# A window attention kernel: order of the LayerNorm transposes, place of the convolution, and the order of the setup

## The chip, the cores and the metric

The kernel runs on one core of one Trainium2 chip. The metric is device time in microseconds (us), the median of the runs. The core has five engines that run their own queues of instructions: TensorE (PE; its weight loads are shown apart as PEld), VectorE (DVE), ScalarE (ACT), GpSimd (POOL) and SyncE (SP, which only issues DMAs here). They meet through semaphores.

## The reference

An image x of 511 x 511 positions with 192 channels (bfloat16) goes through a depthwise 3 x 3 convolution that is added to it, a LayerNorm without weights over the channels, attention with 4 heads of 48 channels in windows of 7 x 7 positions, an output projection, and a residual sum:

```
pe  = sum over i, j of xpad[:, i:i+H, j:j+W, :] * dw_pe[i, j]     # 3 x 3, per channel
x0  = x + pe
h   = (x0 - mean(x0)) / sqrt(var(x0) + 1e-5)
qkv = windows(h) @ w_qkv                    # 73 x 73 windows of 49 tokens
out = softmax(q k^T * 48**-0.5) v           # per window and head
y   = x0 + unwindow(out @ w_o)
```

## The kernel before, in words

**Blocks and groups.** The 5329 windows are cut into 42 blocks of up to 128 windows. In X (three rotating buffers) a window is a partition and its 49 x 192 values lie along it. Attention works on groups of 8 windows: 16 groups in a block, 11 in the last, 667 in all.

**Convolution.** XP holds for each window of a block its 9 x 9 patch, with the 81 positions on the partitions. T holds for each channel an 81 x 49 matrix made of the 9 taps. One matmul per channel (conv_mm, L298) loads the channel's 81 x 128 patch values as weights and streams 49 columns of T. Ten channels fill a psum buffer psc (there are two), and VectorE casts them into X (L303). 192 matmuls make a block.

**LayerNorm.** VectorE adds x itself (ln_add, L310; the rows come by DMA into xs) and takes the statistics (ln_stat, L314). GpSimd makes 1/sqrt (L320, L321) and scales (ln_norm, L329). The mean is taken out through the weights. Then ln_tr (L336 to L355), seven times a block, transposes up to eight positions: for each half of the channels (kt = 0, 1) eight TensorE transposes of 128 x 96 into one of the two banks of a psum buffer ps, and a copy into HO, by VectorE for the first half and by ScalarE for the second.

**Attention of a group.** Stage A makes q and then k with four matmuls of 392 columns each (L364) and a cast on ScalarE (L372). Stage B makes the scores (L402) and the exponential (L410). Stage V makes v with eight matmuls of 192 columns (L380, cast L388). Stage D multiplies with v (L423), and VectorE divides by the sum (L432, L433). Stage E transposes the result back (L447) and copies it over the group's part of HO (L448). D runs one group later than A, E two groups later. proj (L453) multiplies four positions of a finished block with w_o (eight matmuls of 192 columns, L459), ScalarE casts (L463), GpSimd adds to X (L467), and SyncE stores.

**The order.** From the branch on (the logits are shown small enough, or else a slow path runs) the order of each queue is the order in which the Python code issues, so it is written by hand. In the loop over the groups it is: q, E, k, D, the proj calls that are due, ln_tr for the next block if one is due, B, V. While block b is in attention, block b + 1 is prepared: the convolution in the first 44% of the groups, the statistics from 46% to 82%, the transposes from 56% to 96%. The convolution's matmuls are put between others by fill(), which is called after each matmul of q, k, v and proj. It spreads the group's share over nlong calls, 16 plus 8 for each proj. hook() issues statistics, loads and stores. The loads of XP for the block after next begin when the convolution has left XP, from 44% to 92%. All psum work but the convolution takes the three ps buffers in turn, so the fourth user from here waits until the first one's readers are done.

**The setup.** Ahead of the branch, in an order that a scheduler works out from the dependencies, psum, XP and X are cleared, the selection matrix Sel is made by GpSimd, T is made by 49 small matmuls (L120) and copied out two positions at a time with single elements 98 bytes apart (L129), the weights are centred, and a value is computed that decides the branch. After the branch the patches of block 0 are loaded, its convolution runs alone, then its LayerNorm and transposes, and then the loop begins.

## Time and profile before

The time before is 5380.8 us, the median of two runs (5376.48 and 5385.11). The profiled execution has a span of 5361.9 us.

| engine | busy us | share of the span | instructions |
|---|---|---|---|
| TensorE matmuls | 4426.2 | 83% | 75049 |
| TensorE weight loads | 3610.8 | 67% | 75049 |
| ScalarE | 3054.3 | 57% | 3855 |
| VectorE | 2727.6 | 51% | 4190 |
| GpSimd | 2116.4 | 39% | 1188 |

The mean granted clock of TensorE is 0.777 of full speed; in the records it is either 0.50 or 1.00. The main DMA queue's packets take 27.9% of the span of the 16 DMA engines.

The columns: an engine is busy while an instruction of its own runs; a wait on a semaphore is idle time. Weight loads overlap matmuls. A matmul takes longer at the lower clock, so TensorE's busy time depends on its clock. Shares over the whole span are means over stages with different limits, so the stages have to be looked at one by one.

### The profile page before, as it was taken

The page shows a single profiled execution, that of the slowest core. Times are in us where ns is not written, and L with a number is a line of the kernel's source. Part 1 is how long each engine was busy: PE and PEld are TensorE (multiplying, and loading weights), DVE is VectorE, ACT ScalarE, POOL GpSimd, SP SyncE. Part 2 cuts the span into 40 slices and gives each one's busy share as a digit, 9 for nine tenths or more (in the row PEclk, how much of TensorE's full clock was granted, in tenths as well). Part 3 has the DMA queues.
Part 4 walks back from the last instruction along what each step waited for, and adds up shares of the span by engine and source line. Part 5 has one row for each costly group of instructions (what it writes and reads, how often), then busy time and mean ns, then how long its engine had stood idle before and what let it go on. Part 6 is the DMA issues. An engine that isn't in the chain of part 4 may idle for free. (4 is left out here: it accounts for less than half of the span.)

```text
span 5361.9 us, 167300 instructions
## 1 busy us (share of the span) xinstructions
PE 4426.2 (83%) x75049; PEld 3610.8 (67%) x75049; DVE 2727.6 (51%) x4190; ACT 3054.3 (57%) x3855; POOL 2116.4 (39%) x1188
## 2 busy tenths in 40 slices
PE   2688888888888888888888888888888888888777
PEld 1566776776766666677766766666667776676665
DVE  5554555455555544555545555545554555455542
ACT  1455555556555565556655555555555566555555
POOL 3433333334444433334433444433333343344333
PEclk9886787777777776778877777767777888777777
DMA  2222222233333222222323333222222233233221
GB/s 69 59 68 67 68 68 68 68 78 77 82 80 83 72 68 68 68 68 68 78 68 77 83 80 83 71 67 68 68 68 68 68 78 73 70 74 81 68 48 32
DMA packets 529706, 377.00 MB, mean 70 GB/s; under 512 B 454181, under 2 KB 454373, under 8 KB 528979
## 3 DMA queue, kind: packets, MB, share of 16 engines
q1 hardware_dynamic: 528531, 365.92, 27.9%
q8 instruction: 589, 9.65, 0.8%
q14 instruction: 138, 1.13, 0.1%
q10 hardware_dynamic: 448, 0.30, 0.0%
HBM read 265.31 MB, written 100.27 MB: 68 GB/s over the span
## 5 line engine op out<-in xcount | busy, mean ns | idle before, releaser
L467 POOL TENSOR_TENSOR X<-X,pO 128x768 bf16<-128x768 bf16 (+1 forms) x546 | 894.6, 1654 | 2789.2 <-ACT pO L463 2787.9
L364 PE MATMUL ps<-HO,Wqk 96*128 96x392 bf16 x5336 | 1639.4, 426 | 20.1 <-ACT HO L352 15.8
L298 PEld LDWEIGHTS <-XP 81*128 81x128 bf16 x8064 | 1246.8, 185 | 139.2 <-issue 51.6
L298 PE MATMUL psc<-T,XP 81*128 81x49 bf16 x8064 | 1303.1, 211 | 41.3 <-DMA xs<-in_x_dram 32.0
L380 PE MATMUL ps<-Wv,HO 96*128 96x192 bf16 x5336 | 863.4, 299 | 118.3 <-DVE o L433 112.2
L343 PE MATMUL ps<-ident,X 128*96 128x128 bf16 x4116 | 412.0, 253 | 640.9 <-DVE HO L352 592.0
L432 DVE RECIPROCAL rs<-ps 128x16 f32<-128x16 f32 x667 | 169.8, 255 | 1393.8 <-PE ps L423 896.8
L303 DVE CAST X<-psc 128x490 bf16<-128x490 f32 x840 | 542.8, 646 | 591.5 <-PE psc L298 585.0
L364 PEld LDWEIGHTS <-Wqk 96*128 96x128 bf16 x5336 | 623.7, 124 | 303.8 <-issue 238.1
L352 ACT COPY HO<-ps 96x1024 bf16<-96x1024 bf16 (+1 forms) x294 | 284.5, 968 | 869.7 <-PE ps L343 869.7
L343 PEld LDWEIGHTS <-X 128*96 128x96 bf16 x4116 | 336.8, 148 | 644.7 <-issue 598.6
L372 ACT CAST k<-ps 128x784 bf16<-128x784 f32 x667 | 543.6, 815 | 363.8 <-PE ps L364 269.6
L329 POOL TENSOR_TENSOR X<-X,rstd 128x1536 bf16<-128x1536 bf16 (+1 forms) x294 | 734.2, 2515 | 18.5 <-DMA out_dram<-X 5.4
L380 PEld LDWEIGHTS <-HO 96*128 96x128 bf16 x5336 | 604.6, 122 | 158.6 <-issue 111.7
L459 PE MATMUL ps<-Wo,HO 96*128 96x192 bf16 x4116 | 690.6, 302 | 16.3 <-ACT HO L448 12.7
L388 ACT CAST v<-ps 128x768 bf16<-128x768 f32 x667 | 535.7, 803 | 267.3 <-PE ps L380 218.7
L372 ACT CAST q<-ps 128x784 bf16<-128x784 f32 x667 | 543.7, 815 | 249.2 <-PE ps L364 240.9
L433 DVE TENSOR_TENSOR o<-ps,rs 128x768 bf16<-128x768 f32 x667 | 638.4, 957 | 23.4
L459 PEld LDWEIGHTS <-HO 96*128 96x128 bf16 x4116 | 619.1, 180 | 25.2 <-issue 3.5
L463 ACT CAST pO<-ps 128x768 bf16<-128x768 f32 x504 | 401.4, 799 | 392.3 <-PE ps L459 333.4
L447 PEld LDWEIGHTS <-o 128*96 128x96 bf16 x5336 | 526.4, 166 | 104.5 <-issue 45.8
L410 ACT ACTIVATE pt<-ps 128x784 bf16<-128x784 f32 x667 | 550.8, 826 | 62.6 <-PE ps L402 62.5
(55 smaller groups left out, 4068.3 us busy)
## 6 DMA issues: line engine op xcount, KB each, us to landing
XP<-in_x_dram SPq DMA_DIRECT2D x568, 216.0 KB
xs<-in_x_dram SPq DMA_DIRECT2D x574, 168.0 KB
out_dram<-X SPq DMA_DIRECT2D x246, 336.0 KB
XP<-in_x_dram SPq DMA_DIRECT2D x151, 212.6 KB
out_dram<-X SPq DMA_DIRECT2D x82, 168.0 KB
XP<-in_x_dram SPq DMA_DIRECT2D x16, 192.0 KB
XP<-in_x_dram SPq DMA_DIRECT2D x64, 30.4 KB
xs<-in_x_dram SPq DMA_DIRECT2D x63, 23.6 KB
```

Of the source, the lines that this page charges most:

```text
L298: mm(cv.ps[:, (c % 10) * S : (c % 10 + 1) * S], lhsT=XP[0:KP, :, c], rhs=T[0:KP, c, :], start=True, stop=True)
L303: nc.vector.tensor_copy(out=self.X[cv.b % 3][:, :, c0 : c0 + n], in_=cv.ps[:, 0 : n * S].rearrange("p (c s) -> p s c", s=S))
L329: nc.gpsimd.tensor_tensor(out=hbuf(b)[:, s0:s1, :], in0=self.X[b % 3][:, s0:s1, :], in1=rstd[:, i : i + n].unsqueeze(2).to_broadcast([128, ...
L343: mm(pb[0:KT, kt * 1024 + i * 128 : kt * 1024 + (i + 1) * 128], lhsT=h[:, s0 + i, kt * KT : (kt + 1) * KT], rhs=ident[:], start=True, stop ...
L364: mm(ps[:, ab * 512 : ab * 512 + TOK], lhsT=self.Wqk[kt][0:KT, which * 2 + ab, :], rhs=HO[b % 2][0:KT, kt, ck * CH : (ck + 1) * CH, 0:S], ...
L372: nc.scalar.copy(out=dst[:, :, 0:TOK], in_=two_bank(ps, TOK))
L380: mm(ps[:, col : col + C], lhsT=HO[b % 2][0:KT, kt, w : w + 2, :].rearrange("p w s -> p (w s)"), rhs=self.Wv[kt][0:KT, :], start=(kt == 0) ...
L388: eng(out=v_[:].rearrange("p (b j) h e -> p b (j h) e", b=2)[:, :, :, 0:DH], in_=two_bank(ps, 2 * C).rearrange("p b (g d) -> p b g d", d=DH),)
L410: nc.scalar.activation(out=pt[:, 0 : 16 * S].rearrange("p (b n) -> p b n", b=2), in_=two_bank(ps, 8 * S), func=ACTF.Exp, scale=SCALE)
L433: nc.vector.tensor_tensor(out=o_[:].rearrange("p b q (h d) -> p b (q h) d", d=DH), in0=ov[:, :, :, 0:DH], in1=r_[:].rearrange("p (b g) -> ...
L459: mm(ps[:, col : col + C], lhsT=HO[b % 2][0:KT, kt, :, s0 + i], rhs=self.Wo[kt][0:KT, :], start=(kt == 0), stop=(kt == 1))
L467: nc.gpsimd.tensor_tensor(out=xv, in0=xv, in1=o[:, 0:n, :], op=ALU.add)
```

## The change

There are four parts.

1. In ln_tr the transposes of both halves are issued first, and the two copies after them, so that TensorE doesn't meet a copy between its own two batches.
2. fill() takes a weight, 2 after each matmul of q and k, 1 after each of v, and is no longer called in proj. A group's share of the convolution is spread over 24 units (8 matmuls x 2, 8 x 1), so two thirds of it lie beside q and k and one third beside v.
3. The patch loads of block 0 are issued ahead of the branch; load_xp becomes a method for that. XP's clearing is shared by VectorE and GpSimd, X's clearing goes to the end of the setup, and psum's clearing behind Sel. The taps are loaded through ScalarE's queue.
4. T is copied out four positions at a time from both banks of ps, in the order channel, position, so that four neighbouring elements are written together.

The slow path, which doesn't run here, gets a clearing of its own. The diff, cut to its core:

```diff
-        for t in self.PS.t + self.PC.t:
-            nc.vector.memset(t[:], 0.0)
+        self.XP = big.tile([128, BLK, C], BF, name="XP")
+        nc.vector.memset(self.XP[:, 0:88, :], 0.0)
+        nc.gpsimd.memset(self.XP[:, 88:BLK, :], 0.0)
...
-        nc.vector.memset(self.XP[:], 0.0)
-        for t in self.X:
-            nc.gpsimd.memset(t[:], 0.0)
...
-                nc.sync.dma_start(out=dwK[9 * j : 9 * j + 3, :], in_=dw_pe[j])
+                nc.scalar.dma_start(out=dwK[9 * j : 9 * j + 3, :], in_=dw_pe[j])
...
+            make_identity(nc, self.ident[:])
+            for t in self.PS.t + self.PC.t:
+                nc.vector.memset(t[:], 0.0)
-            for n, s0 in enumerate(range(0, S, 2)):
-                ns = min(2, S - s0)
+            for n, s0 in enumerate(range(0, S, 4)):
+                ns = min(4, S - s0)
...
-                dst = self.T[0:KP, :, s0 : s0 + ns].rearrange("p c s -> p s c")
-                src = ps[0:KP, 0 : ns * C].rearrange("p (s c) -> p s c", c=C)
+                if ns == 4:
+                    dst = self.T[0:KP, :, s0 : s0 + ns].rearrange("p c (b s) -> p c b s", b=2)
+                    src = ps[0:KP].rearrange("p (b n) -> p b n", b=2)[:, :, 0 : 2 * C].rearrange("p b (s c) -> p c b s", c=C)
...
+            for t in self.X:
+                nc.gpsimd.memset(t[:], 0.0)
+        for t in self.load_xp(0):
+            t()
         cond = nc.values_load(gi[0:1, 0:1], min_val=0, max_val=1)
...
                         is_transpose=True,
                     )
+            for kt in range(2):
                 eng = nc.vector.tensor_copy if kt == 0 else nc.scalar.copy
                 eng(
...
-                    fill()
+                    fill(2)
...
-                    fill()
+                    fill(1)
...
-        def proj(b, s0, fill):
+        def proj(b, s0):
...
                     mm(ps[:, col : col + C], lhsT=HO[b % 2][0:KT, kt, :, s0 + i], rhs=self.Wo[kt][0:KT, :], start=(kt == 0), stop=(kt == 1))
-                    fill()
...
-        xp = list(load_xp(0))
-        for t in xp:
-            t()
...
-            nlong = 16 + 8 * len(pj)
...
-            def fill():
-                quota[0] += (conv_goal - conv_start) / nlong
+            def fill(weight):
+                quota[0] += (conv_goal - conv_start) * weight / 24
...
-                proj(b - 1, s0, fill)
+                proj(b - 1, s0)
```

## The prediction

> **What bounds the kernel now.** I read the page first. TensorE is busy 83% of the span, no other engine above 57%, so I asked what TensorE's other 17%, 936 us, waits for. The page's groups (columns: busy us, mean ns | idle us just before the group, and who ended it) give one answer, and the list of waits (total us, times, longest us) counts it:

> ```profile
> L343 PE MATMUL ps<-ident,X 128*96 128x128 bf16 x4116 | 412.0, 253 | 640.9 <-DVE HO L352 592.0
> L352 ACT COPY HO<-ps 96x1024 bf16<-96x1024 bf16 (+1 forms) x294 | 284.5, 968 | 869.7 <-PE ps L343 869.7
> ```
> ```profile
> PE ps L343 <- DVE HO L352: 592.0, 294, 8.8
> PE ps L380 <- DVE o L433: 112.2, 43, 2.8
> ```

> 294 is 42 blocks x 7 calls of ln_tr: every call stops TensorE once, 2.0 us on average, and these stops are two thirds of its idle time. The timeline of one group shows how:

> ```profile
> 2249.69 0.85 PE L343 MATMUL ps<-ident,X 128*96 128x128 bf16 x8
> 2249.87 0.26 DVE L432 RECIPROCAL rs<-ps 128x16 f32<-128x16 f32 x1 [6.44 <-issue]
> 2250.16 0.96 DVE L433 TENSOR_TENSOR o<-ps,rs 128x768 bf16<-128x768 f32 x1
> 2251.04 1.21 DVE L352 COPY HO<-ps 96x1024 bf16<-96x1024 bf16 x1
> 2252.30 0.61 PE L343 MATMUL ps<-ident,X 128*96 128x128 bf16 x8 [1.76 <-DVE HO L352]
> 2252.95 1.01 ACT L352 COPY HO<-ps 96x1024 bf16<-96x1024 bf16 x1 [2.84 <-PE ps L343]
> ```

> The second eight transposes wait for VectorE's copy of the first eight, and that copy stands in VectorE's queue behind attention work (L432, L433). ScalarE idles meanwhile.

> The windows view, one window per group of a block (from one q cast to the next; columns: length, busy us of PE, PEld, DVE, ACT, POOL with counts, granted clock, DMA share, GB/s), shows where TensorE is not the limit and what its clock does. These are groups 7, 8, 9, 11, 13 and 15 of 16:

> ```profile
> 2191.49:2197.81 6.32, 6.32 (x127) 5.75 (x125) 3.70 (x6) 4.56 (x7) 2.64 (x2) 1.00 0.02 6
> 2197.81:2202.30 4.49, 4.35 (x102) 3.45 (x100) 2.52 (x5) 3.72 (x7) 1.83 (x2) 1.00 0.63 157
> 2202.30:2209.69 7.39, 4.38 (x97) 3.51 (x96) 7.25 (x13) 4.58 (x7) 2.06 (x2) 0.97 0.55 127
> 2218.41:2227.81 9.40, 7.34 (x109) 5.53 (x108) 6.64 (x10) 5.29 (x8) 9.32 (x6) 0.68 0.57 147
> 2238.05:2247.13 9.08, 7.10 (x107) 5.06 (x106) 2.81 (x4) 4.97 (x6) 8.84 (x6) 0.69 0.53 127
> 2255.78:2264.79 9.01, 7.04 (x107) 5.28 (x106) 2.34 (x3) 4.97 (x7) 0.00 (x0) 0.69 0.00 0
> ```

> The start is read from the timeline's first lines:

> ```profile
> 18.31 0.98 SPq L98 DMA_DIRECT2D dwK<-in_dw_pe_dram  x3
> 32.42 1.18 PE L120 MATMUL ps<-dwK,Sel 21*81 21x192 bf16 x6 [32.42 <-POOL Sel L107]
> 59.80 23.48 SPq L267 DMA_DIRECT2D XP<-in_x_dram  x18
> 88.98 17.39 PE L298 MATMUL psc<-T,XP 81*128 81x49 bf16 x192 [32.03 <-DMA xs<-in_x_dram]
> 171.08 0.53 PE L364 MATMUL ps<-HO,Wqk 96*128 96x392 bf16 x1
> ```

> Sel is late behind 23.8 us of X memsets on GpSimd, the patches are asked for only after the branch, and 171 us pass before the first q.

> [...] the sharp limit above counts transposes as busy; without them windows at 40 to 70% went both ways. [...] 384 single elements 98 bytes apart took 2.16 us, 5.6 ns each, where L352 writes runs of eight at 1.2 ns (1024 in 1.22 us).

> **The change part by part.**

> *Transposes before copies.* No instruction is added. Sixteen transposes run through, then both copies start, each waiting for PE only. What TensorE now meets next: the score stage, which needs the k cast (done); v, whose psum buffer is free when L433 ends, 1.45 us after stage D; then q of the next group, whose buffer is ln_tr's own (rotation of three), so it waits for both copies. At full clock, from the end of D: transposes to 1.0 us (eight take 0.65 with a 0.2 tail, so 0.064 each), scores to 1.45, v to 2.3; the copy ends at 1.45 + 1.21 = 2.7 plus a semaphore, plus whatever statistics VectorE has queued before it. So without statistics (groups 13 to 16) about 0.6 us is left of the 2 us stop; with them (11, 12) VectorE's queue is the bound.

> What the groups then take: group 8 shows the stages without transposes or convolution, at full clock: 4.35 us of TensorE with one projection (0.8). With transposes and no projection that is 4.5; ScalarE needs 4.97; the chain above closes at about 5.3. If TensorE idles 0.6 to 0.8 us per 3.4 us window it is above 75% and keeps full clock. I allow a quarter of the time at half clock, and take 6.1 for groups 13 to 15, and 7.4 for group 16, which has a second, short transpose whose copies the next block's first q must wait for. Groups 11 and 12 are held by VectorE, 6.6 and 6.4 us busy; with gaps 7.8 and 7.4. Group 9 stays, group 10 (8.72, full at half clock) gives 0.5. Groups 11 to 16 take 9.40 + 10.24 + 9.08 + 8.65 + 9.01 + 11.05 = 57.4 us in this block; 7.8 + 7.4 + 3 x 6.1 + 7.4 = 40.9 after. With group 10 that is 17 us a block, and 41 blocks carry such transposes: **-697 us**.

> *Convolution only beside q, k, v.* The same 27.4 matmuls a group, 18.3 in q and k (2.3 per matmul), 9.1 in v, none in proj. Full-clock timelines: q alone has 0.17 us per matmul, 0.20 with one convolution matmul, 0.295 with two; v 0.084, 0.122, 0.205; proj 0.10 and 0.18. Before, with one proj: 8 x 0.043 + 8 x 0.05 + 8 x 0.093 = 1.5 us a group for the convolution; after: 8 x 0.15 + 8 x 0.05 = 1.6. [...] So +0.1 x 7 groups x 41 = **+30 us**[...].

> *Start.* XP's memset is split, 7.1 us on VectorE (88/128 of 10.3) beside 6.5 on GpSimd (7680 elements at the 0.84 ns of L203), and X's memsets move behind Sel, so Sel is there at about 15 instead of 32. T: 13 copies of 768. The trace has no runs of four; at 1.2 ns an element one takes 0.9 us[...]. I take 1.2, since each run is as long as half of L352's. With both engines taking turns T is ready near 27 (before 55) and the branch value 4 later, 31 (before 59). Patch loads start near 8.5 instead of 59.8 and land after the same 29 us, at 38, hidden behind T. The branch may wait for X's memsets, to 39; after it VectorE's own memsets (12.2 us before, 60.1 to 72.3) come ahead of the first convolution cast. So the convolution runs effectively from about 50 instead of 89. What follows to the first q is the same work: **-40 us**, between -30 and -50.

> Sum: 5380.8 - 697 + 30 - 40 = **4674 us**.

> **Rivals.**
> *The clock doesn't follow.* The stops go, but TensorE keeps its mean of 0.68 in groups 11 to 16 and is simply full: 7.34 + 7.35 + 7.10 + 6.89 + 7.04 + 7.88 = 43.6 us plus 0.3 each, 45.4, saves 12 x 41 = 492: 4879. For it: half clock also came at the end of bursts by VectorE. Against: a full TensorE rose to full clock in 278 of 476 windows.
> *The wait moves.* The next q waits for the copy that TensorE used to wait for, VectorE's queue being the same. Half of the 492 is left: about 5125. Against: 2.34 us of VectorE in groups 14 and 15.
> *More than that.* Groups 13 to 15 run at 5.3, and blocks begin at full clock; 8 of the first 41 blocks (by their q casts) now take some 132 instead of 122.5 because their convolution begins at half clock. 2.4 + 2.5 us more a block, 200 us: about 4475.
> *Slower.* Nine convolution matmuls in each of q, k and v fill a psc buffer (ten) faster than VectorE empties two: 20 fills a block at 0.65 us, 13 x 41 = 533; and all blocks get the slow beginning, 10 x 33 = 330; against -492 - 40 this gives 5712. For it: nothing more than that VectorE is queued; L298 idles now 9 us after the start, and VectorE is busy 3.7 of 6.3 us in group 7.

> **How the numbers follow.** Forecast 0.50, clock not following 0.27, more 0.11, wait moves 0.08, slower 0.04. The first three lie between 4475 and 4880; with the unknowns of the start and of the convolution (some 40 us) and part of the fourth case left out, 4465 to 4960. Only "slower" is above 5488; "moved" can lose enough to end within 2%: faster 0.93, same 0.03, slower 0.04.

> **What would show it.** L343's idle near nothing, L352's wait on ScalarE down from 869.7; groups 13 to 15 near 6 us with a clock above 0.85; a new wait of q (L364) on the HO copies, under 1 us a call; convolution groups within 0.3 us; first q near 130. It is wrong if TensorE's mean clock stays at 0.78, or if L364 or L402 shows some 1.5 us of idle per transpose.

## The result, and the profile after

The changed kernel takes 4885.9 us (median of two runs, 4854.8 and 4917.0) against 5380.8 before: a ratio of 0.908, with a 95% interval from 0.883 to 0.933. The forecast was 4674 us, inside a range of 4465 to 4960; of the 707 us forecast, 495 came. Of all runs below, one was over 1.5% slower than the fastest of its kernel, at a lower clock (4466.4 us, of the changed kernel with its transposes in the psc buffers); it is left out of that kernel's time.

The stop is gone from the transposes, and something else has come. The page's groups of the changed kernel, for the lines that were L343, L364 and L352:

```profile
L375 PE MATMUL ps<-HO,Wqk 96*128 96x392 bf16 x5336 | 1603.9, 390 | 325.0 <-ACT HO L363 267.0
L363 ACT COPY HO<-ps 96x1024 bf16<-96x1024 bf16 (+1 forms) x294 | 285.1, 970 | 619.5 <-DVE HO L363 538.6
```

The answer on the groups (same columns) has the transposes' own line:

```profile
L353 PE MATMUL ps<-ident,X 128*96 128x128 bf16 x4116 | 324.9, 239 | 141.7 <-ACT HO L363 52.5 <-POOL X L339 48.9 <-ACT HO L459 27.5
```

The transposes had 640.9 us of idle time and kept 141.7. But q (L375) now waits 325.0 us, where it had 20.1, and ScalarE's copy waits for VectorE's copy, 538.6 us in 250 waits. Before, ScalarE's wait was put down to TensorE alone. The line of q before:

```profile
L364 PE MATMUL ps<-HO,Wqk 96*128 96x392 bf16 x5336 | 1639.4, 426 | 20.1 <-ACT HO L352 15.8
```

The windows, one per group, of a block near the middle, groups 7, 8, 9, 11, 13 and 15 as in the prediction:

```profile
1956.81:1963.00 6.19, 6.19 (x129) 5.72 (x129) 3.53 (x6) 4.59 (x7) 2.10 (x2) 1.00 0.04 10
1963.00:1967.49 4.49, 4.35 (x102) 3.46 (x100) 2.52 (x5) 3.71 (x6) 2.36 (x2) 1.00 0.63 157
1967.49:1975.99 8.50, 5.49 (x97) 4.18 (x96) 7.75 (x13) 4.59 (x8) 2.49 (x4) 0.83 0.54 133
1981.59:1990.93 9.34, 6.34 (x103) 4.67 (x101) 8.31 (x13) 5.01 (x8) 9.26 (x6) 0.78 0.53 132
1999.31:2005.91 6.60, 4.78 (x106) 3.65 (x104) 4.67 (x8) 4.56 (x7) 4.36 (x3) 1.00 0.70 172
2012.24:2018.57 6.33, 4.74 (x106) 3.57 (x104) 2.44 (x3) 4.57 (x7) 0.00 (x0) 1.00 0.00 0
```

Group 15 now runs at full clock throughout. Its TensorE work shrank from 7.04 to 4.74 us by the clock alone (107 matmuls before, 106 after; in both traces q's matmuls, where they run back to back, start 0.17 us apart at full clock and 0.33 at half), but the group takes 6.33 us, so 1.6 us of idle is left. The timeline of that group shows where:

```profile
2013.86 1.05 PE L353 MATMUL ps<-ident,X 128*96 128x128 bf16 x16 [0.23 <-ACT HO L459]
2014.04 0.96 DVE L444 TENSOR_TENSOR o<-ps,rs 128x768 bf16<-128x768 f32 x1
2015.02 1.22 DVE L363 COPY HO<-ps 96x1024 bf16<-96x1024 bf16 x1
2016.27 1.01 ACT L363 COPY HO<-ps 96x1024 bf16<-96x1024 bf16 x1 [1.76 <-DVE HO L363]
2017.18 0.82 ACT L421 ACTIVATE pt<-ps 128x784 bf16<-128x784 f32 x1
2017.33 0.84 PE L375 MATMUL ps<-HO,Wqk 96*128 96x392 bf16 x4 [1.28 <-ACT HO L363]
```

The sixteen transposes end at 2014.9. L444, which began while they ran, VectorE's copy and ScalarE's copy follow one another without a pause, and q, whose buffer it is, starts when the last has ended. The exponential (L421) stands behind that copy in ScalarE's queue.

The start, from the timeline's first lines:

```profile
9.75 22.17 SPq L234 DMA_DIRECT2D XP<-in_x_dram  x18
14.86 2.85 PE L118 MATMUL ps<-dwK,Sel 21*81 21x192 bf16 x16 [14.86 <-POOL Sel L102]
44.76 15.49 PE L308 MATMUL psc<-T,XP 81*128 81x49 bf16 x172 [6.62 <-DVE X L313]
122.22 0.51 PE L375 MATMUL ps<-HO,Wqk 96*128 96x392 bf16 x1 [1.80 <-DVE HO L363]
```

The first q comes at 122.2 instead of 171.1 us.

The mean time of a block's parts, over blocks 2 to 40 of the profiled execution, from one q cast to the next, helps to place the rest:

| groups of a block, us | before | changed |
|---|---|---|
| 1 to 8 (convolution) | 50.7 | 51.2 |
| 9 to 16 (statistics, transposes) | 73.9 | 62.3 |
| mean clock over the run | 0.777 | 0.853 |

### The profile page after: what moved, and what is told of

Read it like the earlier page. It is cut to its first block, busy times and chain, and to the rows that moved or that the text cites. A ratio compares the mean times of both kernels' runs of the same rounds, so it can differ in the third digit from the quotient of the medians.

```text
span 4853.1 us, 167074 instructions
## 1 busy us (share of the span) xinstructions
PE 4049.1 (83%) x75049; PEld 3356.1 (69%) x75049; DVE 2771.4 (57%) x4184; ACT 2965.4 (61%) x3849; POOL 2129.7 (44%) x1189
## 5 line engine op out<-in xcount | busy, mean ns | idle before, releaser
L375 PE MATMUL ps<-HO,Wqk 96*128 96x392 bf16 x5336 | 1603.9, 390 | 325.0 <-ACT HO L363 267.0
L308 PEld LDWEIGHTS <-XP 81*128 81x128 bf16 x8064 | 1114.5, 176 | 171.4 <-issue 78.8
L308 PE MATMUL psc<-T,XP 81*128 81x49 bf16 x8064 | 1103.3, 224 | 41.5 <-DMA XP<-in_x_dram 33.1
L375 PEld LDWEIGHTS <-Wqk 96*128 96x128 bf16 x5336 | 634.2, 122 | 544.3 <-issue 419.3
L391 PE MATMUL ps<-Wv,HO 96*128 96x192 bf16 x5336 | 716.5, 265 | 153.9 <-DVE o L444 137.4
L363 ACT COPY HO<-ps 96x1024 bf16<-96x1024 bf16 (+1 forms) x294 | 285.1, 970 | 619.5 <-DVE HO L363 538.6
L444 DVE TENSOR_TENSOR o<-ps,rs 128x768 bf16<-128x768 f32 x667 | 638.7, 958 | 23.7
L391 PEld LDWEIGHTS <-HO 96*128 96x128 bf16 x5336 | 532.9, 109 | 162.8 <-issue 128.2
L421 ACT ACTIVATE pt<-ps 128x784 bf16<-128x784 f32 x667 | 551.1, 826 | 65.3 <-PE ps L413 65.3
L324 DVE BATCH_NORM_STATS2 bnst<-X 128x6 f32<-128x384 bf16 x1050 | 530.2, 548 | 7.3
L458 PEld LDWEIGHTS <-o 128*96 128x96 bf16 x5336 | 474.0, 151 | 76.2 <-issue 20.4
L458 PE MATMUL ps<-ident,o 128*96 128x128 bf16 x5336 | 510.8, 251 | 1.4 <-DVE o L444 1.4
L470 PE MATMUL ps<-Wo,HO 96*128 96x192 bf16 x4116 | 478.9, 267 | 19.1 <-ACT HO L459 15.3
L470 PEld LDWEIGHTS <-HO 96*128 96x128 bf16 x4116 | 427.9, 181 | 26.3 <-issue 3.7
```

The lines of the kernel that those rows point to most:

```text
L308: mm(cv.ps[:, (c % 10) * S : (c % 10 + 1) * S], lhsT=XP[0:KP, :, c], rhs=T[0:KP, c, :], start=True, stop=True)
L324: nc.vector.bn_stats(out=bnst[:, i, :], in_=self.X[b % 3][:, s : s + 2, :].rearrange("p s c -> p c s"))
L375: mm(ps[:, ab * 512 : ab * 512 + TOK], lhsT=self.Wqk[kt][0:KT, which * 2 + ab, :], rhs=HO[b % 2][0:KT, kt, ck * CH : (ck + 1) * CH, 0:S], ...
L391: mm(ps[:, col : col + C], lhsT=HO[b % 2][0:KT, kt, w : w + 2, :].rearrange("p w s -> p (w s)"), rhs=self.Wv[kt][0:KT, :], start=(kt == 0) ...
L421: nc.scalar.activation(out=pt[:, 0 : 16 * S].rearrange("p (b n) -> p b n", b=2), in_=two_bank(ps, 8 * S), func=ACTF.Exp, scale=SCALE)
L444: nc.vector.tensor_tensor(out=o_[:].rearrange("p b q (h d) -> p b (q h) d", d=DH), in0=ov[:, :, :, 0:DH], in1=r_[:].rearrange("p (b g) -> ...
```

## The experiments

Every ratio is to runs of the kernel before on the same chip.

**The parts alone.** The change was taken apart: only the order of the transposes; only the convolution's place; only the setup; and all but the convolution's place.

> The kernel before with only the transposes of both halves ahead of the copies. Theory A (the gain is the transposes' order, stop and clock together; in the trace of the changed kernel groups 9 to 16 of a block are 11.6 us shorter, 41 blocks): 5381 - 476 = about 4905 us, clock about 0.85. Rival B (the convolution's new place carries part of it, by making TensorE's work denser so that the clock holds): above 5000.

> The kernel before with only the convolution moved beside q, k and v. Theory A: groups 1 to 8 changed by +0.6 us a block in the trace, so 5381 + 25 = about 5405, at most 60 either way. Rival B: below 5300.

> The kernel before with only the new setup (patch load ahead of the branch, memsets moved, T in longer copies). The first q came at 122.2 instead of 171.1 us in the changed kernel. Theory A: the steady blocks are untouched, 5381 - 49 = about 5332. Rival: the first blocks lose it again to another wait, 5370 or more.

> The changed kernel with the convolution spread as before (proj too). Theory A: 25 us faster than the changed kernel or the same, 4830 to 4890. Rival B: above 4950, because the convolution's place is part of the gain.

The edits are those of the diff above. For the first, the whole of it is

```diff
+            for kt in range(2):
                 eng = nc.vector.tensor_copy if kt == 0 else nc.scalar.copy
```

| kernel | us | ratio, 95% interval | groups 1 to 8 | groups 9 to 16 | blocks begun at half clock |
|---|---|---|---|---|---|
| before | 5380.8 | | 50.7 | 73.9 | 9 of 39 |
| transposes only | 4937.6 | 0.919 (0.914 to 0.923) | 52.8 | 62.2 | 29 |
| convolution only | 5464.2 | 1.017 (1.011 to 1.024) | 52.7 | 74.0 | 17 |
| setup only | 5324.2 | 0.991 (0.988 to 0.994) | 50.1 | 73.8 | 6 |
| all but the convolution | 4913.9 | 0.915 (0.909 to 0.920) | 52.1 | 62.4 | 26 |
| changed | 4885.9 | 0.908 (0.883 to 0.933) | 51.2 | 62.3 | 22 |

(The last column counts blocks with a mean clock under 0.53 in groups 1 and 2.) The order of the transposes carries the gain, about 440 us, and the setup 55. Theory A had these within 33 us. The convolution's place is another matter. Alone it costs about 90 us, where A had 25 and B a gain, so both miss; in the changed kernel it may save 28, which these intervals don't tell from nothing, and 4913.9 lies between the ranges of A and B. In both pairs, with the place changed and not, groups 1 to 8 go with the number of blocks that begin at half clock. That is where the 11.6 us of groups 9 to 16 are partly given back: the blocks of the kernels with reordered transposes begin at half clock more often.

**Is the clock a cause?** The kernel before was left in its old order, and unread matmuls were put into the stop:

```diff
                 eng(
                     out=HO[b % 2][0:KT, kt, :, s0 : s0 + N],
...
+                if kt == 0:
+                    junk = PCB.next()
+                    for _ in range(7):
+                        mm(junk[:], lhsT=self.Wqk[0][0:KT, 0, :], rhs=self.Wqk[1][0:KT].rearrange("p m n -> p (m n)"), start=True, stop=True)
```

> The kernel before, order of transposes and copies as it was, with seven matmuls of 512 columns that nobody reads between the two batches of transposes, into a psc buffer that is free then. TensorE still waits for the copy, but with work in the gap: 1.5 us of it at full clock, 3.0 at half. Theory A (the stop costs twice, its time and the clock that falls with it): the clock stays up in groups 11 to 16, groups 13 to 15 go from 8.9 to about 7, 9.6 us a block, about 4990 us in all. Rival (a stop costs its length and the clock is a bystander): at half clock the added work is longer than the stop, 5380 to 5500 us.

It takes 4804.4 us, ratio 0.890 (0.886 to 0.894): the kernel before, with 495 us of work added that nobody needs, is faster by 11%. The added work took 1.68 us a call; the 0.17 and 0.33 us of q's 392 columns give, as an estimate, 1.55 us for seven matmuls of 512 columns at full clock and 3.0 at half. The windows of groups 13 and 15, and the group of lines of the added matmuls:

```profile
1993.26:2000.15 6.89, 6.37 (x113) 4.27 (x111) 4.24 (x7) 4.57 (x7) 5.21 (x3) 1.00 0.69 168
2007.03:2013.91 6.88, 6.37 (x113) 4.28 (x111) 2.34 (x3) 4.57 (x8) 0.00 (x0) 1.00 0.01 2
```
```profile
L359 PE MATMUL psc<-Wqk,Wqk 96*128 96x512 bf16 x2058 | 494.9, 380 | 0.0
```

The clock is 1.00 where it was 0.69, and a group takes 6.9 us where it took 9. Groups 9 to 16 go from 73.9 to 63.8 us, and groups 1 to 8 from 50.7 to 47.2 although nothing was added there; one block in 39 begins at half clock instead of nine. TensorE's wait for VectorE's copy, 592.0 us before, is still 149.8. Theory A holds, and was too timid; the rival falls.

**What holds the next q?** Two edits of the changed kernel: ScalarE's copy issued first, and one ScalarE copy of both halves.

```diff
-            for kt in range(2):
+            for kt in (1, 0):
                 eng = nc.vector.tensor_copy if kt == 0 else nc.scalar.copy
```
```diff
-            for kt in range(2):
-                eng = nc.vector.tensor_copy if kt == 0 else nc.scalar.copy
...
+            nc.scalar.copy(
+                out=HO[b % 2][0:KT, :, :, s0 : s0 + N],
+                in_=pb[0:KT].rearrange("p (k n) -> p k n", k=2)[:, :, 0 : N * 128].rearrange("p k (s w) -> p k w s", w=128),
+            )
```

> The changed kernel with the copy of the second half (ScalarE) issued ahead of that of the first (VectorE). Theory A (the two copies run one after the other because they read one ps buffer, in the order of issue): now VectorE's copy waits for ScalarE's, the chain is as long as before, 4850 to 4920 us, groups 14 and 15 at 6.2 to 6.4. Rival (ScalarE's copy came late for another reason): the copies overlap, groups at 5.3, about 4750.

> The changed kernel with one ScalarE copy of both halves (2048 elements) in place of two copies. Theory A (q of the next group waits for the chain of L444, VectorE's copy and ScalarE's copy): the copy starts right behind the transposes and takes some 1.9 us, no VectorE in the chain; groups 14 and 15 about 6.0, groups 11 and 12 about 1 us shorter as VectorE loses 1.2 us of work: about 4800. Rival (ScalarE becomes the bound): no gain, 4880 or more.

With ScalarE first it takes 4763.1 us, 0.883 (0.879 to 0.888). The copies still run one after the other, now the other way round; the answer on its groups:

```profile
L363 DVE COPY HO<-ps 96x1024 bf16<-96x1024 bf16 (+1 forms) x294 | 337.1, 1147 | 210.2 <-ACT HO L363 209.9
L363 ACT COPY HO<-ps 96x1024 bf16<-96x1024 bf16 (+1 forms) x294 | 284.1, 967 | 228.6 <-PE ps L353 228.6
```

So the mechanism of A is right (the second copy waits for the first, in the order of issue), but its time is not: the gain is about that of the rival. Group 15 takes 5.87 us on average, not 6.2 to 6.4, and the larger gains lie in groups 12 and 13, 1.2 and 1.3 us each. A likely reason, not tested apart: ScalarE's copy no longer stands behind L444 and VectorE's copy, and what is queued behind it on ScalarE, the exponential and the v and q casts, comes earlier. With one copy it takes 4706.3 us, 0.873 (0.869 to 0.877), and groups 14 and 15 come to 6.0 and 5.9 us: A's reason held, and its 4800 was too high.

**Is it the shared buffer?** The halves go into the two psc buffers, which are free when transposes run; first in the changed kernel, whose edit is shown, then in the kernel before with its old order of copies.

```diff
-            ps = PS.next()
-            pb = ps[:].bitcast(BF)
+            pbs = [PCB.next()[:].bitcast(BF) for _ in range(2)]
...
-                        pb[0:KT, kt * 1024 + i * 128 : kt * 1024 + (i + 1) * 128],
+                        pbs[kt][0:KT, i * 128 : (i + 1) * 128],
```

> The changed kernel with the two halves transposed into the two psc buffers, which the convolution has left by then, in place of a ps buffer. Theory A (the copies wait for each other, and q for both, because of the shared ps buffer): both waits go, groups 13 to 15 at 5.0 to 5.3, about 4650 us. Rival (the copies wait for each other because both write HO): ScalarE still waits for VectorE, groups stay near 6, 4780 or more.

> The kernel before, in its old order (transposes of one half, its copy, transposes of the other, its copy), with the two halves in the two psc buffers in place of one ps buffer. Theory A (the stop comes from the shared buffer, the order only decides who waits): no stop, about as fast as the changed kernel with psc, plus 55 for the old start: 4430 to 4530 us. Rival (the order itself is what counts): the stop stays, 5000 or more.

The changed kernel with psc takes 4418.1 us, 0.816 (0.811 to 0.821); the kernel before with psc takes 4428.1 us, 0.823 (0.818 to 0.829). The rivals fall in both. The first is well below theory A's 4650, though groups 13 to 15, at 7.0, 5.2 and 4.75 us on average, are not all where A put them. Two lines of the timeline of the first, group 14, and its group 15 as a window:

```profile
1806.39 1.01 ACT L362 COPY HO<-psc 96x1024 bf16<-96x1024 bf16 x1 [0.24 <-PE psc L352]
1806.74 1.21 DVE L362 COPY HO<-psc 96x1024 bf16<-96x1024 bf16 x1
```
```profile
1808.70:1813.44 4.74, 4.66 (x106) 3.48 (x104) 2.34 (x3) 4.56 (x7) 4.24 (x5) 1.00 0.56 135
```

Here the copies overlap, and group 15 is down to 4.74 us with TensorE full at full clock. In the kernel before with psc the order is the old one; its transposes:

```profile
L342 PE MATMUL psc<-ident,X 128*96 128x128 bf16 x4116 | 298.5, 226 | 82.3 <-POOL X L329 63.8 <-DVE HO L351 17.9 <-ACT HO L351 0.4
```

Their idle time is 82.3 us, of which 18.3 are for a copy. So the stop of 592 us came from the shared buffer, and the order of the code only decides who waits. Each half has its own 1024 elements with ps and with psc alike; what these two edits take away is that the halves share a buffer, and with that the transposes' waits for copies go, in the kernel before, from 592.0 us to 18.3. The psc buffers do a second thing: they take the transposes out of the rotation of the three ps buffers, so that q no longer meets their buffer. What part of the 468 us against the changed kernel comes from that alone is not shown.

**Where the last half clock comes from.** Unread matmuls at the block's end in the changed kernel; and in the kernel with psc the same, with ten more in group 9. Here junk(k) issues k matmuls of 512 columns into a psc buffer.

```diff
                     if f == 1.0:
+                        junk(5)
                         while n.tr < 7:
                             n.transpose(7, -9.0)
+                        junk(6)
...
+                if n and f0 == 0.5:
+                    junk(10)
```

> The changed kernel with matmuls of 512 columns that nobody reads at the end of each block, five ahead of the last short transposes and six behind them, where TensorE waits for copies. Theory A (groups 1 and 2 of a block take 14.65 instead of 11 us because the block's end leaves the clock at half): groups 1 and 2 fall to 11 to 12 us, 41 blocks x 3, about 4760 us. Rival (they are slow for another reason, such as the loads or the convolution's place): 4870 to 4930, since the added work takes 1 to 2 us a block.

> The kernel with transposes into the psc buffers, plus the same unread matmuls at the block's end, and ten of them in group 9, where TensorE waits for VectorE's statistics. Theory A (what is left of half clock comes from these two idle places): groups 1, 2, 10 and 11 shrink by some 4 us a block, about 4260 us, mean clock above 0.95. Rival (the gaps come back elsewhere, or the work delays group 9): 4400 or more.

The first takes 4698.4 us, 0.873 (0.868 to 0.878), and only one block in 39 begins at half clock, where it was 22. Groups 1 to 8 take 47.3 us instead of 51.2, and groups 9 to 16 are unchanged (62.0): 3.9 x 41 = 160 us, where the medians differ by 188 and the two profiled executions by 155. So the giveback at the start of blocks was the clock, and came from the idle end of the block before. The second is a miss: 4390.2 us, 0.816 (0.811 to 0.821), not 4260. Groups 1 to 8 fall from 49.8 to 47.1, but groups 9 to 16 rise from 53.4 to 54.6. Groups 9 and 10 together win 2.6 us and 11 and 12 lose 2.9, and group 16, with the added work of the block's end, takes 10.15 instead of 8.45. So the time comes back elsewhere, as the rival says, though its 4400 isn't reached.

**The convolution's place, once more.** The kernel with psc, with the convolution spread as before:

> The changed kernel with transposes into the psc buffers, and the convolution spread as before (proj too). It leaves out only the second part of the change. Theory A (with the stop gone the convolution's new place is a loss: in the traces groups 1 to 8 take 49.7 us with it, 48.3 in the kernel before with psc; and the new setup is worth 55): 4350 to 4385 us. Rival (the difference in groups 1 to 8 is chance in how a block falls against the clock's windows): 4410 to 4450, as with the new place.

It takes 4377.1 us (4376.4 to 4380.3), 0.813 (0.809 to 0.818), where theory A put it and outside the rival's 4410. But its interval overlaps with that of the kernel with the new place (0.811 to 0.821), so the 41 us between the medians are likely and not shown. Against the kernel before with psc, this kernel has the new order of the transposes and the new setup, and is 51 us faster, where the setup alone gave 55: with the buffers apart, nothing that shows is left for the order to give. With the whole change but its second part, and with the buffers apart, it has the lowest median of all kernels here, 19% below the one before.

## Why the prediction was right, and where it was not

**What bounds the kernel.** Right. The stops and the clock that they pull down were the main cost, and both moved. That 4886 lies inside the range is owed to the rivals that widened it, not to the sum, which is 212 us off. That a stop costs twice was the reading that mattered most: filling it without removing it gave 576 us, more than the change's 495.

**The clock.** What was counted in the trace before came again in the trace after, as far as full clock goes: of its windows at full clock (3.413 us, the step of its clock records too), all 140 with TensorE busy under 55% were followed by half clock, all 657 above 75% by full clock. These counts take transposes as busy: with both kinds of transposes left out, 154 windows of the trace after with under 55% busy were followed by full clock. The counts are no rule: with the filled stop, one of 51 windows under 55% kept full clock and six of 1070 above 75% lost it; and at half clock, where none of 223 windows under 95% rose before, 3 of 163 did after. "The clock doesn't follow" came nearest in time (4879) and was wrong in its mechanism, since the mean clock rose from 0.777 to 0.853, in groups 11 to 16 from 0.68 to 0.85. It was the clock more than the stop that gave the gain: of the 11.1 us by which these groups shrank in a block, 8.7 are less busy time of TensorE for the same work (43.2 to 34.5 us), and only 2.4 are less idle time (15.0 to 12.7).

**Transposes before copies.** The direction was right, the size was not: 440 us (transposes only) where 697 were forecast. The step that failed reads "then both copies start, each waiting for PE only". ScalarE's copy waits for VectorE's. In the trace before, it always came after TensorE's second batch, so this wait couldn't be seen there, and I took the copies to be independent. The chain therefore closes not with the copy's end at 2.7 us after stage D and 0.6 us of idle, but after ScalarE's copy, 1.01 us later, and with ScalarE's queue held up behind it. Groups 11 to 16 take 8.8, 8.2, 7.9, 6.7, 6.4 and 9.2 us, 47.2 in all, where 40.9 were forecast: 6.3 x 41 = 258 us too little. The block that the forecast was read from was 0.9 us shorter there than the mean one (58.3 us), so the gain fell short by 5.4 us a block, 221 us. The new order alone also made groups 1 to 8 longer, 50.7 to 52.8 us. The largest misses are groups 13 and 16, 1.8 us each. In group 16 the short last transposes wait for ScalarE's copy as well: L353's 52.5 us are in 41 waits, 1.3 us in each block.

**More waits, in part.** The rival in which the wait moves to the next q also came true in part: where 592.0 us stood between the transposes, 325.0 stand before q, 305.3 of them for the two copies. That is 1.04 us for each of 294 calls, just over the 1 us that the prediction named as its sign. Its other signs came in part: the transposes' idle time is 141.7 us and not near nothing, ScalarE's wait fell from 869.7 to 619.5, and groups 13 to 15 take 7.9 to 6.4 us, with a clock of 0.88.

**The start of blocks.** The forecast left groups 1 and 2 as they were. They take 14.6 us instead of 13.5, as more blocks begin at half clock; filling the block's end took this away.

**Convolution.** Right in its arithmetic at full clock, and too small a term for what it does. Groups 1 to 8 of the blocks whose groups 1 to 8 run at full clock throughout took 46.87 us in the kernel with psc and the new place (mean of 8 blocks), and 46.61 in the kernel with psc and the old one (14 blocks). That is +0.26, where 0.73 was forecast. That alone it costs about 90 us, with 17 blocks begun at half clock instead of 9, I had only at the edges; why the new place lets more blocks begin so is not shown.

**Start.** Right: -40 forecast; the first q is 49 us earlier, and the setup alone gave 55. T's copies of 768 took 1.10 us (1.2 taken), and the branch value was there at 31.0 (31 forecast). The convolution was held by VectorE's memsets after the branch until 44.8, not 50.

## What to carry to other kernels

When a wait is taken away, ask which dependency made it: if it is a shared buffer, a new order can hand the wait to the next user of the buffer (592.0 us before the transposes became 325.0 before q), and separate buffers can end it (here they left 18.3 us of the 592.0). Read TensorE's idle time together with its clock, stage by stage, because a short stop in each group can cost more by the clock than by its length (here 8.7 us of a block's gain were less busy time, 2.4 less idle time). A wait that never came last in the trace before can still be there (ScalarE's for VectorE's copy, 538.6 us in the trace after), so list what an instruction would wait for next, its buffer's other reader included.

## What was not expected of the hardware

Work that nobody reads made the kernel faster: 2058 matmuls, 495 us of TensorE, took the time from 5380.8 to 4804.4 us, with the mean clock going from 0.777 to 0.942. And stops of 1.8 to 2.0 us, once in a group of 9 us, were enough to hold the mean clock near 0.69; with work in them it was 1.00.
